# RWKV-7 attention and an exact-GELU MLP on one core: the first three chunks' a, v and r are turned on TensorE instead of VectorE, and the work ahead of the main loop is put in another order

## The chip, the cores and the metric

The kernel runs on one core of a Trainium2 chip. The time is device time in microseconds (us) of the whole launch; lower is better. Before the change it is 798.99 us, the median of 3 runs (798.1 to 800.18).

## The reference, cut to what matters

For each of 4 batches and 8 heads a 40 by 40 state is carried over 768 time steps; the result then goes through an MLP of width 2048.

```python
for t in range(S):                                   # S = 768, D = 40
    y[:, :, t] = einsum('bhd,bhde->bhe', rt, state)
    Sa = einsum('bhde,bhe->bhd', state, at)
    state = state * wt[:, :, None, :] - outer(Sa, bt) + outer(vt, kt)
x = y.transpose(0, 2, 1, 3).reshape(B * S, H * D)    # 3072 x 320
h = x @ w_in                                         # w_in 320 x 2048
out = gelu_exact(h) @ w_out                          # w_out 2048 x 320
```

## The kernel before, in words

Time is cut into 12 chunks of 64 steps (c = 0 to 11). In a chunk the recurrence is solved as matrix products over all 32 batch-heads: decays are accumulated (`sums`: cum, wT_ps), b and k are scaled by them (`scale_b` into nb, `scale_k` into ks), and then come the products of pairs of time steps: N from a and b, A from a and k, RV from r and v, M from r and the solved sa. Each is masked to its triangle by a VectorE multiplication out of PSUM (`masked`, L467). N needs an inverse of a triangular matrix. This is done in blocks of 32 (`start_inverse`): N is masked, written to DRAM by four DMAs (L504), read back in another layout by two (L547), inverted column by column by 62 small operations (L561, L562) on VectorE for chunk 0 and on GpSimd for the others, written to DRAM (`store_inverse`, L574) and read back (`fetch_inverse`, L584 and L588) into Tt and T2. Then `corner` (L, J) and `joined` (J2) complete the inverse; `make_X`, `make_sa`, `make_saT`, `make_M` and `make_QY` (QY) give the chunk's output and the next state, and `outputs` brings the output into the MLP's layout (xt) with eleven small DMAs.

The MLP of a chunk (`mlp`) is cut into eight pieces that `fill` puts between the steps of the next chunk's recurrence: four ph pieces (xt times w_in, L748, then GELU) and four po pieces (times w_out, L756).

Both weights come in 64-bit floats as pairs of 32-bit words, and are made into 32-bit floats on the chip (`to_float`, L263 to L282) piece by piece: five pieces for each half of w_in, sixteen for w_out. VectorE, ScalarE and GpSimd share a piece, or VectorE does most of it alone. `first_load` and `second_load` bring the words; `convert` and `seconds` put the pieces between other steps. The raw words lie in buffers that are needed later (w_out_sb, gt, spare_raw), so loads wait for conversions. The first two ph pieces need the first half of w_in, the next two the second half; the first po piece needs w_out's pieces 0 to 7.

All engines work their instructions in the order in which the program is written (`manual_schedule`); nothing reorders them. Chunks 0 to 2 are written out by hand ahead of the loop (L807 to L976), since they run beside the loading and the converting of the weights; chunks 2 to 11 then go through the loop of L978. DMAs are issued by the queue of SP or of ScalarE, also in program order: a DMA that waits holds back all that stands behind it on its queue.

The a, v and r of a chunk must be turned so that time runs along the free axis. Before, `fetch_pairs` (L146 to L162) loads them as pairs of steps in overlapping pieces of 72 and 48 elements, so that VectorE's 32 by 32 block transposes (`turn`, L164 to L167) give the turned form; that is four DMAs for a, eight for v and eight for r. v is loaded a second time as plain rows (`load_VR`, L181), for use as a right-hand side. b and k after scaling are turned on TensorE (`flip`, L387) and copied out of PSUM by ScalarE (L434, L446). The `warm` matmuls between steps (L801) compute nothing that is used.

Of the kernel before, what the change touches and what calls it, by code (L numbers as in the profile page):

```python
# [10 lines left out]
FP32 = mybir.dt.float32  # L11
UINT32 = mybir.dt.uint32
ALU = mybir.AluOpType
# [6 lines left out]
def kernel(  # L20
# [82 lines left out]
    def ring(name, n, shape, zero, eng):  # L103
        tiles = []
        for i in range(n):
            t = const.tile(shape, FP32, name=f"{name}{i}")
            if zero is not None:
                eng.memset(zero(t), 0.0)
            tiles.append(t)
        turn = [0]  # L110

        def take():
            turn[0] += 1
            return tiles[(turn[0] - 1) % n]
        return take
# [5 lines left out]
        return t  # L121


    def unused(t):
        for x in range(2):
            nc.gpsimd.memset(t[x * HP + BL:(x + 1) * HP, :, BW - BL:D + BL], 0.0)
# [3 lines left out]
    VR_ring = ring("VR", 2, [P, 2, G, NP, VC], None, None)  # L130


    raws = {}
# [30 lines left out]
    def turn(to, c, n):  # L164

        nc.vector.transpose(to.rearrange("p n (s y) -> p n y s", y=2),  # L166
                            raws.pop((c, n)).rearrange("p n (y d) -> p n y d", y=2)[:, :, :, :BL])  # L167

    def load_w(c, t=None, eng=nc.sync):
        t = w_tile if t is None else t  # L170
        fetch(c, "w", w, eng, t[:, :G * DM].rearrange("p (g h d) -> p g h d", g=G, h=H))
        raws[c, "w"] = t

    def load_a(c, t=None, eng=nc.sync):
        fetch_pairs(c, "a", a, eng, False, t)

    def load_kb(c):
        fetch(c, "b", b, nc.sync)
# [31 lines left out]
    load_w(1, early_w)  # L210
    fetch(1, "b", b, nc.sync, ahead["b"])
    load_a(1, early_a)
    for t in (*paired.values(), early_a):
        unused(t)

    one = const.tile([P, 1], FP32, name="one")
    nc.vector.memset(one, 1.0)
# [18 lines left out]
        nc.gpsimd.memset(wp_ring()[:, :, 0], 1.0)  # L236
    ks_ring, nb_ring = (ring(n, 2, [P, G, H, HP], pads, nc.gpsimd) for n in ("ks", "nb"))
    Tt_ring = ring("Tt", 1, [P, 2, G, NP, C], whole, nc.gpsimd)

    part_ring, avs_ring = (ring(n, 1, [P, 2, DM + REST], lambda t: t[:, :, DM:], nc.gpsimd) for n in ("part", "avs"))  # L240

    def flat(t):
        return t.rearrange("p j g n t -> p (j g n) t")
# [158 lines left out]
        return t.rearrange("p g n (e t) -> p g n e t", e=2)  # L402

    def turn_a(c):
        aT = turned_in.setdefault(c, {})["aT"] = work.tile([P, 2, G, NP, C], FP32, tag="aT", name="aT", bufs=2)
        turn(aT.rearrange("p e g i t -> p (e g i) t"), c, "a")

# [14 lines left out]

    def scale_a(c):
        t = turned_in[c]
        aT = t["aT"]
        wp = t["wp"].rearrange("p (n e) t -> p e n t", e=2)[:, :, :, :C]
        flat_a = aT.rearrange("p e g i t -> p e (g i) t")
        nc.vector.tensor_tensor(flat_a, flat_a, wp, ALU.mult)
        t["aT"] = aT.rearrange("p e g i t -> p g i e t")

    def turn_b(c):
# [17 lines left out]
    def turn_v(c):  # L449
        t = turned_in[c]  # L450
        vT = side("vT", "late", 1)
        turn(vT.rearrange("p q m (e t) -> p (q m e) t", e=2), c, "v")
        t["vT"] = parts(vT)

    def turn_r(c):
        rT = side("rT", "rT", 2)
        turn(rT.rearrange("p q m (e t) -> p (q m e) t", e=2), c, "r")
        turned_in[c]["rT"] = parts(rT)

    def turns_b(c):  # L460
# [5 lines left out]
    def masked(to, pt):  # L466
        nc.vector.tensor_tensor(to, pt, upper.unsqueeze(1).to_broadcast([P, 2 * G * NP, C]), ALU.mult)  # L467
# [37 lines left out]
                                  in_=flat(N)[at:at + BL, :, z * BL:(z + 1) * BL])  # L505
        blocks[c] = blk

    def make_RV(c):
        t = turned_in[c]
        masked(flat(t["VR"])[:, :, D:], products("RV_ps", t["vT"], t["rT"], False))  # L510

    def make_A(c, mask=True):
        t = turned_in[c]
# [299 lines left out]
    make_N(0)  # L813
    logs(1)
    sums(1)
    warm(3, 3)
    scale_b(1)
    turn_a(1)
    scale_a(1)
    inverse = start_inverse(0, nc.vector)  # L820
    turn_b(1)
    fetch(0, "k", k, nc.sync)
    for _ in range(5):
        next(inverse)
    make_N(1)
    scale_k(0)

    spare_x = work.tile([P, NK, TB], FP32, tag="xt", name="spare_x").rearrange("p k t -> p (k t)")
    st_ring()
# [1 line left out]
    spare_w = spare_st.rearrange("p e i g d -> p (e i g d)")  # L831
    nw = BL // 2 * BL
    run(start_inverse(1, nc.gpsimd, (spare_x[:, :BL * BL], spare_w[:, :nw], spare_w[:, nw:])))
    turn_k(0)
    make_A(0, False)
    fetch(1, "k", k, nc.sync, ahead["k"])
    load_w(2, None, nc.scalar)
    first_load(False, 0, early(0, 4))
    load_a(2, None, nc.scalar)
    fetch(2, "b", b, nc.scalar)  # L840
    load_v(0)
    load_r(0, nc.scalar)
    load_VR(0)
# [10 lines left out]
    turn_k(1)  # L854
    turn_r(0)
    make_RV(0)
    make_A(1, False)
    warm(4, 4, 4, 4)
    load_VR(1)
    first_load(True, 0, early(4))  # L860
    corner(0)
    warm(2)
    joined(0)
    warm(2)
    make_X(0)
    make_sa(0)
    mask_A(1)
    make_saT(0)
    warm(2)
    first_pieces((0, 1, 2), 0, nc.gpsimd)  # L870
    convert(1)
    make_y2(0)
    make_M(0)
    first_load(False, 2, early(5, 4))
    store_inverse(1)
    fetch_inverse(1)
    nc.gpsimd.memset(spare_st.rearrange("p e i g d -> p (e i g) d")[:, :, D:], 0.0)
    convert(1, True)
    warm(2)
    make_QY(0)  # L880
    outputs(0)
    pieces.append(mlp(0))
    make_av(1)
    convert(1)
    first_pieces((3,), 0, nc.vector)
    first_pieces((4,), 0, nc.gpsimd)
    corner(1)
    turn_state()
    convert(1)
    joined(1)  # L890
    convert(1, True)
    make_X(1)
    sums(2)

    first_load(False, 3)
    for f in range(4):
        second_load(f, 2 * f)
    first_load(True, 1, spare_raw[:, :LW])
    make_sa(1)
    make_saT(1)  # L900
    scale_b(2)
    turn_a(2)
    scale_a(2)
    first_pieces(range(NK), 1, nc.gpsimd)
    convert(1)
    fill()
    turn_b(2)
    convert(1)
    load_r(1)
    load_v(1)  # L910
    fetch(2, "k", k, nc.sync)
    convert(1)
    fill()
    make_N(2)
    convert(1)
    turn_r(1)
    make_y2(1)
    make_M(1)
    convert(1, True)
    turn_v(1)  # L920
    make_RV(1)
    for f in range(4, 8):
        second_load(f, 2 * f)
    scale_k(2)
    run(start_inverse(2, nc.gpsimd))
    second_load(8, 0, spare_raw)
    second_load(9, 2, spare_raw)

# [6 lines left out]
    make_QY(1)  # L935
    outputs(1)
    pieces.append(mlp(1))
    load_VR(2)
    load_v(2)
    load_r(2)  # L940
    load_w(3)
    seconds(6)
    turn_v(2)
    turn_r(2)
    make_RV(2)
    make_A(2)
    fill()
    load_a(3)
    load_kb(3)
    seconds(0, (10, 12))  # L950
    make_av(2)
    logs(3)
# [2 lines left out]
    turn_a(3)  # L955
    scale_a(3)
    turn_state()
    load_VR(3)
    load_v(3)
    load_r(3)  # L960
    seconds(1, (11, 14))
    fill()
    seconds(1, (12, 0, spare_raw), (13, 2, spare_raw))
# [2 lines left out]
    fetch_inverse(2)  # L966
    seconds(2, (14, 14))
    seconds(1, (15, 0, spare_raw))
    seconds(2, last=True)
    fill()  # L970
    make_N(3)
# [92 lines left out]
```

## Time and profile before

| | us |
|---|---|
| median of 3 runs | 798.99 |
| the profiled execution, whole | 802.02 |
| its span (first to last instruction) | 800.3 |
| TensorE busy in the span | 697.4 |
| VectorE, ScalarE, GpSimd busy | 280.3, 214.5, 312.0 |

The profiled execution lies 3.0 us above the median; 1.7 us of it lie outside the span. In the profile PE is TensorE's matmuls, PEld its weight loads, DVE VectorE, ACT ScalarE, POOL GpSimd; SPq and ACTq are the queues of SP and ScalarE that issue DMAs. A line such as L467 is a line of the kernel. A timeline row gives start, duration, engine, line, operation, the tile written and the tile read, with the number of instructions merged into it; in square brackets is the idle time ahead of it and what ended that. The granted TensorE clock is a share of full speed.

### The profile page before, as it was taken

What the parts mean: (1) busy time and instruction counts of PE and PEld (TensorE: products, weight loads), DVE (VectorE), ACT (ScalarE), POOL (GpSimd) and SP (SyncE); (2) the same over time, 40 slices, a digit from 0 to 9 for tenths busy, and PEclk for the clock granted to TensorE, in tenths of its full rate; (3) what the DMA queues carried; (4) which work ended last, traced back from release to release, by engine and by line L of the source; (5) the groups of instructions that cost most, each with busy time, mean ns of one, the idle gap of its engine ahead of it and who ended that gap; (6) DMA issues with size and microseconds to landing.
All of it is one profiled execution on the core that took longest, in us unless ns stands there. A gap on an engine that the chain in (4) does not pass through costs nothing.

```text
span 800.3 us, 30351 instructions
## 1 busy us (share of the span) xinstructions
PE 697.4 (87%) x13666; PEld 557.9 (70%) x13666; DVE 280.3 (35%) x425; ACT 214.5 (27%) x258; POOL 312.0 (39%) x778
## 2 busy tenths in 40 slices
PE   7207774628599999999999999999999999999997
PEld 4205664525388788787887887877878878878684
DVE  3742646584612414314234124143142341311000
ACT  5112453214123233134232332331332322102020
POOL 4183326841056066074281470650742824700000
PEclk9659786958699999999999999999999999999999
DMA  8798375086372472553643724724635432020100
GB/s 129 131 159 168 70 180 145 19 135 132 83 136 50 73 137 55 106 99 67 120 79 66 142 52 72 138 57 93 111 69 115 82 68 51 17 51 2 26 9 17
DMA packets 275178, 70.28 MB, mean 88 GB/s; under 512 B 263432, under 2 KB 268328, under 8 KB 275048
## 3 DMA queue, kind: packets, MB, share of 16 engines
q1 hardware_dynamic: 264032, 66.24, 43.4%
q10 hardware_dynamic: 11016, 2.10, 1.7%
q8 instruction: 107, 1.75, 0.9%
q14 instruction: 23, 0.19, 0.1%
HBM read 54.13 MB, written 10.22 MB: 80 GB/s over the span
## 4 chain that ended last, share of the span: by engine, by line
PE 80%; DMA 6%; DVE 4%; SPq 4%; issue 2%; ACT 2%; DVEq 0%; ACTq 0%
PE ph L748 27%; PE po L756 26%; PE QY L100 6%; PE J L100 2%; PE sap L100 2%; PE RV_ps L100 2%; PE M_ps L100 2%; PE saT_ps L100 2%; PE av L100 2%; PE N_ps L100 1%; PE kT_ps L392 1%; PE A_ps L100 1%; PE cum L100 1%; PE X L100 1%; DMA b_raw<-in_b_dram 1%
## 5 line engine op out<-in xcount | busy, mean ns | idle before, releaser
L756 PE MATMUL po<-w_out_sb,gt 128*128 128x320 f32 x768 | 223.2, 444 | 11.2 <-DVE w_out_sb L276 9.4
L748 PE MATMUL ph<-xt,w_in_sb 64*128 64x256 f32 x1920 | 223.2, 384 | 2.6 <-issue 2.5
L748 PEld LDWEIGHTS ph<-xt,w_in_sb 64*128 64x128 f32 x1920 | 185.2, 189 | 25.8 <-issue 4.1
L756 PEld LDWEIGHTS po<-w_out_sb,gt 128*128 128x128 f32 x768 | 144.5, 194 | 73.2 <-DVE w_out_sb L276 13.2
L561 POOL TENSOR_TENSOR tmp<-W,Nb 128x126 f32<-128x126 f32 (+22 forms) x310 | 112.2, 362 | 171.9 <-DMA Nb<-N 148.3
L562 POOL TENSOR_TENSOR W<-W,tmp 128x126 f32<-128x126 f32 (+22 forms) x310 | 117.0, 377 | 24.3
L750 ACT ACTIVATE gt<-ph 128x1024 f32<-128x1024 f32 x48 | 49.1, 1024 | 166.7 <-PE ph L748 166.6
L760 DVE COPY os<-po 128x320 f32<-128x320 f32 x24 | 11.8, 492 | 109.5 <-PE po L756 109.5
L467 DVE TENSOR_TENSOR SM<-M_ps,upper 128x1024 f32<-128x1024 f32 x12 | 14.7, 1225 | 74.3 <-PE M_ps L100 74.3
L100 PE MATMUL RV_ps<-rT,vT 40*64 40x64 f32 x768 | 15.6, 236 | 25.9 <-DVE rT L166 21.5
L705 DVE TENSOR_TENSOR xt<-QY,wpT 128x512 f32<-128x512 f32 x24 | 15.5, 686 | 61.5 <-PE QY L100 61.5
L100 PE MATMUL av<-VR,A 64*64 64x40 f32 x768 | 14.4, 234 | 24.9 <-DVE A L467 24.9
L417 POOL TENSOR_TENSOR ks<-k_raw,part 128x640 f32<-128x640 f32 x10 | 16.2, 1624 | 50.7 <-DMA r_pairs<-in_r_dram 20.4
L545 POOL MEMSET W<- 128x512 f32 x10 | 5.3, 530 | 74.9 <-DMA inv<-W 74.9
L100 PEld LDWEIGHTS av<-VR,A 64*64 64x64 f32 x768 | 13.1, 142 | 29.5 <-DVE A L467 25.1
L100 PEld LDWEIGHTS RV_ps<-rT,vT 40*64 40x64 f32 x768 | 13.9, 149 | 27.8 <-issue 26.4
L627 DVE COPY Tt<-J 32x512 f32<-32x512 f32 x12 | 8.3, 689 | 71.3 <-ACT Tt L627 71.3
L446 ACT COPY kT<-kT_ps 128x1024 f32<-128x1024 f32 x12 | 12.1, 1012 | 71.3 <-PE kT_ps L392 71.3
L467 DVE TENSOR_TENSOR VR<-RV_ps,upper 128x1024 f32<-128x1024 f32 x12 | 14.7, 1224 | 46.9 <-PE RV_ps L100 46.9
L268 ACT ACTIVATE power<-power,rebias 128x320 uint32<-128x320 uint32 (+1 forms) x26 | 16.2, 624 | 49.2 <-DVE power L267 49.2
L467 DVE TENSOR_TENSOR A<-A_ps,upper 128x1024 f32<-128x1024 f32 x12 | 14.7, 1223 | 39.9 <-PE A_ps L100 39.9
L529 ACT COPY avs<-av 128x640 f32<-128x640 f32 x12 | 8.3, 694 | 64.7 <-PE av L100 58.3
(136 smaller groups left out, 881.1 us busy)
## 6 DMA issues: line engine op xcount, KB each, us to landing
Nb<-N SPq DMA_DIRECT2D x22, 256.0 KB
VR<-in_v_dram SPq DMA_DIRECT2D x24, 160.0 KB
out_dram<-os SPq DMA_DIRECT2D x48, 80.0 KB
k_raw<-in_k_dram SPq DMA_DIRECT2D x22, 160.0 KB
w_out_sb<-in_moe_w_out_dram SPq DMA_DIRECT2D x11, 320.0 KB
v_pairs<-in_v_dram SPq DMA_DIRECT2D x48, 72.0 KB
w_tile<-in_w_dram SPq DMA_DIRECT2D x20, 160.0 KB
b_raw<-in_b_dram SPq DMA_DIRECT2D x20, 160.0 KB
```

Of the source, the lines that this page charges most:

```text
L100: nc.tensor.matmul(o, lhsT, rhs, start=first, stop=True, skip_group_check=True)
L268: nc.scalar.activation(power, power, ACT.Relu, bias=rebias, scale=8.0)
L417: eng.tensor_tensor(ks[:, :, :, :D], raws.pop((c, "k")), rwv, ALU.mult)
L446: nc.scalar.copy(kT, flip(by_pair(t["ks"]), "kT_ps"))
L467: nc.vector.tensor_tensor(to, pt, upper.unsqueeze(1).to_broadcast([P, 2 * G * NP, C]), ALU.mult)
L561: eng.tensor_tensor(t, views[0], views[1], ALU.mult)
L562: eng.tensor_tensor(views[2], views[2], t, ALU.add)
L705: nc.vector.tensor_tensor(xt[:, :NP, g * P:(g + 1) * P].rearrange("p i (e t) -> p i e t", e=2), Y, wp[:, g, :, :, :C], ALU.mult)
L748: nc.tensor.matmul(ph[:, x, s], w_in_sb[half(x), kt, p * P:(p + 1) * P], xt[half(x), kt], start=kt == 0, stop=kt == NK - 1)
L750: nc.scalar.activation(gt[:, 4 * q:4 * q + 4].rearrange("p (x s) t -> p x s t", x=2), ph, ACT.Gelu)
L756: nc.tensor.matmul(po[:, g], gt[:, f, g * P:(g + 1) * P], w_out_sb[:, f], start=f == 0, stop=f == NF - 1)
L760: nc.vector.tensor_copy(os, po[:, g])
```

## The change

For chunks 0 to 2 (`NT = 3`) a and r are loaded as plain rows, padded to 64 columns a head, and turned by `flip` on TensorE; v is not loaded a second time, but turned on TensorE from the rows that `load_VR` brings (16 matmuls with the identity). a's scaling by the decay reads PSUM directly; v and r are copied out of PSUM by ScalarE. r of chunk 1 goes into v's buffer. The zeroing of columns that this needs is done on GpSimd at the start, and the old buffers' unused parts are zeroed later (`unused`: four memsets on GpSimd, two on VectorE).

The steps ahead of the loop are put in another order: k of chunks 0 and 1 is loaded with w, b and a at the start; chunk 1's N is masked before the first inverse's columns rather than after five of them; r, v rows and w of the next chunks go to SP's queue instead of ScalarE's; A and RV of chunk 0 are multiplied before the first inverse ends, and masked after it; the loads of w_in, the conversions, and chunk 1's and 2's v and r stand at other places. Of the ten `warm` matmuls one stays, of 384 columns.

```diff
+    NT = 3
     def load_a(c, t=None, eng=nc.sync):
-        fetch_pairs(c, "a", a, eng, False, t)
+        if c < NT:
+            fetch(c, "a", a, eng, by_64(paired["a"] if t is None else t).rearrange("p (g h) d -> p g h d", g=G))
+        else:
+            fetch_pairs(c, "a", a, eng, False, t)
...
     def load_v(c):
-        fetch_pairs(c, "v", v, nc.sync, True)
+        if c >= NT:
+            fetch_pairs(c, "v", v, nc.sync, True)
 
     def load_r(c, eng=nc.sync):
-        fetch_pairs(c, "r", r, eng, True)
+        if c >= NT:
+            fetch_pairs(c, "r", r, eng, True)
+            return
+        t = by_64(paired["v" if c == 1 else "r"]).rearrange("p (h g) d -> p h g d", g=G)
+        for e in range(2):
+            for g in range(G):
+                eng.dma_start(out=t[half(e), :, g, :D],
+                              in_=r[G * e + g, :, c * C:(c + 1) * C].rearrange("h t d -> t h d"))
+        raws[c, "r"] = t
...
     load_a(1, early_a)
+    fetch(0, "k", k, nc.sync)
+    fetch(1, "k", k, nc.sync, ahead["k"])
...
     def turn_v(c):
+        if c < NT:
+            pt = duo("vT_ps").rearrange("p q (m t) -> p q m t", m=NP)
+            for q in range(2):
+                for m in range(NP):
+                    for g in range(G):
+                        mm(pt[half(g), q, m], t["VR"][:, g, q, m, :HP], ident)
+            nc.scalar.copy(vT, pt)
...
     def turn_r(c):
+        if c < NT:
+            raw = raws.pop((c, "r"))
+            nc.scalar.copy(rT, flip(lambda q, m: raw[:, NP * q + m].rearrange("p g d -> p (g d)"), "rT_ps"))
...
     run(inverse)
     queues = nc.sync, nc.scalar
     store_inverse(0, queues)
+    load_VR(1)
+    first_pieces((0,), 0, nc.vector)
+    convert(1)
     fetch_inverse(0, queues)
-    first_load(False, 1)
-    turn_v(0)
-    scale_k(1, nc.vector)
     mask_A(0)
+    mask_RV(0)
     make_av(0)
...
+    load_w(3)
+    load_kb(3)
+    load_VR(3)
+    unused(paired["r"], nc.vector)
+    load_a(3)
+    seconds(6)
     fill()
```

Three places where the order of instructions moves. First SP's queue, from behind chunk 1's second transfer of N (spare_x) to the first inverse's write (inv). This is how it stands before; w_out_sb is here the raw buffer of w_in's words, and SP has only one of the two inv transfers, ScalarE's queue has the other:

```order
L143 DMA early_k<-in_k_dram 64x16x40 x2
L330 DMA w_out_sb<-in_moe_w_in_dram 64x4x512
L330 DMA w_out_sb<-in_moe_w_in_dram 64x3x512
L332 DMA w_out_sb<-in_moe_w_in_dram 40x512
L333 DMA w_out_sb<-in_moe_w_in_dram 24x512
L158 DMA v_pairs<-in_v_dram 32x8x72 x2
L158 DMA v_pairs<-in_v_dram 32x8x48 x2
L158 DMA v_pairs<-in_v_dram 32x8x72 x2
L158 DMA v_pairs<-in_v_dram 32x8x48 x2
L184 DMA VR_70<-in_v_dram 64x16x40 x2
L574 DMA inv<-W 1024x1x32
```

The same queue in the changed kernel, between the same two transfers:

```order
L191 DMA VR_131<-in_v_dram 64x16x40 x2
L204 DMA r_pairs<-in_r_dram 64x8x40 x4
L144 DMA w_tile<-in_w_dram 64x16x40 x2
L353 DMA w_out_sb<-in_moe_w_in_dram 64x4x512
L353 DMA w_out_sb<-in_moe_w_in_dram 64x3x512
L355 DMA w_out_sb<-in_moe_w_in_dram 40x512
L356 DMA w_out_sb<-in_moe_w_in_dram 24x512
L353 DMA w_out_sb<-in_moe_w_in_dram 64x4x512
L353 DMA w_out_sb<-in_moe_w_in_dram 64x3x512
L355 DMA w_out_sb<-in_moe_w_in_dram 40x512
L356 DMA w_out_sb<-in_moe_w_in_dram 24x512
L622 DMA inv<-W 1024x1x32
```

The eight small loads of v pairs are gone, r and w have come over from ScalarE's queue, and a second group of w_in's words stands in front of the inverse's write; before, that group stood behind its read.

Second, VectorE behind the first inverse's last column (W). Before:

```order
L562 TENSOR_TENSOR W<-W,tmp 128x16
L166 STREAM_TRANSPOSE vT<-v_pairs 128x16x2x32
L417 TENSOR_TENSOR ks_130<-early_k,avs_140 128x16x40
L467 TENSOR_TENSOR A<-A_ps,upper 128x1024
L166 STREAM_TRANSPOSE rT<-r_pairs 128x16x2x32
L467 TENSOR_TENSOR VR_70<-RV_ps,upper 128x16x64
L597 STREAM_TRANSPOSE L<-Tt_136 128x512
```

In the changed kernel:

```order
L610 TENSOR_TENSOR W<-W,tmp 128x16
L290 TENSOR_SCALAR power<-w_out_sb 128x512
L292 TENSOR_SCALAR mant<-w_out_sb 128x512
L509 TENSOR_TENSOR A<-A_ps,upper 128x1024
L509 TENSOR_TENSOR VR_131<-RV_ps,upper 128x16x64
L295 SCALAR_TENSOR_TENSOR power<-w_out_sb,power 128x512
L298 SCALAR_TENSOR_TENSOR mant<-w_out_sb,mant 128x512
L299 SCALAR_TENSOR_TENSOR w_in_sb<-mant,power 128x512
L509 TENSOR_TENSOR A<-A_ps,upper 128x1024
L645 STREAM_TRANSPOSE L<-Tt_129 128x512
```

The transposes and chunk 1's scaling of k are gone from here, and a conversion of w_in stands in two parts around chunk 0's masks; it reads the words of both groups of loads above.

Third, VectorE from chunk 1's output (xt, st) to chunk 2's masks (VR, A), where w_out's pieces (power, mant) stand. The seven rows below are the changed kernel's; before, six pieces and the two transposes of v and r stood between the last st row and the VR row:

```order
L753 TENSOR_TENSOR xt<-QY,wpT_118 128x4x128 x2
L775 TENSOR_TENSOR st_74<-QY,st_72 128x8x40
L776 TENSOR_TENSOR st_74<-st_74,wpT_118 128x8x40
L775 TENSOR_TENSOR st_74<-QY,st_72 128x8x40
L776 TENSOR_TENSOR st_74<-st_74,wpT_118 128x8x40
L509 TENSOR_TENSOR VR_131<-RV_ps,upper 128x16x64
L509 TENSOR_TENSOR A<-A_ps,upper 128x1024
```

The masks come first now, and the six pieces behind them; on TensorE the first po piece of chunk 0 still stands directly behind chunk 2's A.

More of the change, by code (lines that the diff above doesn't have):

```diff
@@ L404, in turn_a @@
     def turn_a(c):
+        if c < NT:
+            turned_in.setdefault(c, {})["a_ps"] = flip(by_pair(raws.pop((c, "a"))), "aT_ps")
+            return
         aT = turned_in.setdefault(c, {})["aT"] = work.tile([P, 2, G, NP, C], FP32, tag="aT", name="aT", bufs=2)
@@ L815 @@
     sums(1)
-    warm(3, 3)
+    scale_k(0)
+    inverse = start_inverse(0, nc.vector)
     scale_b(1)
@@ L819 @@
     scale_a(1)
-    inverse = start_inverse(0, nc.vector)
+    warm(3)
     turn_b(1)
-    fetch(0, "k", k, nc.sync)
-    for _ in range(5):
-        next(inverse)
+    scale_k(1)
     make_N(1)
-    scale_k(0)
     spare_x = work.tile([P, NK, TB], FP32, tag="xt", name="spare_x").rearrange("p k t -> p (k t)")
@@ L833 @@
     run(start_inverse(1, nc.gpsimd, (spare_x[:, :BL * BL], spare_w[:, :nw], spare_w[:, nw:])))
+    load_VR(0)
+    load_r(0)
+    load_w(2)
+    first_load(False, 0, early(0, 4))
+    first_load(False, 1)
     turn_k(0)
     make_A(0, False)
[L836 to L843, printed above, removed]
+    turn_v(0)
+    turn_r(0)
+    make_RV(0, False)
+    turn_k(1)
     logs(2)
@@ L903 @@
     scale_a(2)
-    first_pieces(range(NK), 1, nc.gpsimd)
     convert(1)
@@ L919 @@
     convert(1, True)
[L920 to L924, printed above, removed]
+    for n in "av":
+        unused(paired[n], nc.gpsimd)
     run(start_inverse(2, nc.gpsimd))
+    load_VR(2)
+    load_r(2)
     second_load(8, 0, spare_raw)
```

106 lines of the change are left out of this document (56 added, 50 removed).

## The prediction

> **What bounds the kernel now.** I first read the page, to see where TensorE is not busy.
>
> ```profile
> span 800.3 us, 30351 instructions
> PEclk9659786958699999999999999999999999999999
> PE 80%; DMA 6%; DVE 4%; SPq 4%; issue 2%; ACT 2%; DVEq 0%; ACTq 0%
> ```
>
> Four fifths of the chain that ended last are TensorE, and its granted clock is full in all slices but the first eleven. Next I cut the span into stages (us from the start; busy us and instructions of PE, PEld, DVE, ACT, POOL; granted clock; DMA share; GB/s). The cuts are where TensorE begins chunk 0's av (58.8), ends chunk 0's QY (87.5), begins chunk 1's sap (103.2), begins the third ph piece (138.4), ends chunk 1's QY (152.9), begins chunk 2's av (184.3) and ends chunk 3's turning of k (219.5).
>
> ```profile
> 25.00:58.80 33.80, 3.99 (x76) 3.40 (x76) 21.96 (x67) 3.03 (x3) 18.36 (x45) 0.50 0.88 148
> 58.80:87.50 28.70, 23.63 (x684) 18.24 (x684) 9.88 (x14) 7.32 (x12) 12.26 (x27) 0.82 0.73 138
> 87.50:103.20 15.70, 8.42 (x332) 7.01 (x325) 12.61 (x18) 6.83 (x12) 6.09 (x5) 0.89 0.44 95
> 103.20:138.40 35.20, 22.32 (x472) 20.23 (x472) 18.14 (x23) 17.11 (x24) 13.51 (x12) 0.74 0.62 151
> 138.40:152.90 14.50, 14.32 (x221) 12.05 (x216) 6.44 (x14) 4.50 (x6) 12.29 (x31) 0.92 0.12 44
> 152.90:184.30 31.40, 9.88 (x146) 7.54 (x146) 23.21 (x40) 3.37 (x6) 15.62 (x36) 0.62 0.69 120
> 184.30:219.50 35.20, 22.86 (x254) 15.16 (x254) 19.73 (x44) 11.52 (x15) 2.98 (x4) 0.75 0.45 98
> 219.50:794.40 574.90, 572.82 (x11221) 462.61 (x11220) 158.77 (x196) 148.51 (x168) 222.13 (x590) 1.00 0.40 75
> ```
>
> From 219.5 us on TensorE is busy for 572.8 of 574.9 us. The change edits nothing behind that point, so what counts is how much earlier chunk 3's turning of k ends. Ahead of it TensorE waits (waits of TensorE up to 220 us: total, times, longest):
>
> ```profile
> PE av L100 <- DVE A L467: 24.9, 1, 24.9
> PE RV_ps L100 <- DVE rT L166: 21.5, 1, 21.5
> PE po L756 <- DVE w_out_sb L276: 9.4, 5, 5.7
> PE QY L100 <- DVE rT L166: 6.4, 1, 6.4
> PE RV_ps L100 <- DVE vT L166: 4.4, 1, 4.4
> ```
>
> Four of the five name VectorE's work on chunks 0 to 2, and the change touches these four.
>
> **Step 1, to the first J.** The timeline around the first inverse:
>
> ```profile
> 21.91 1.16 PE L100 MATMUL N_ps<-aT,nT 40*64 40x64 f32 x64 [1.16 <-DVE W L548]
> 24.89 0.19 DVE L561 TENSOR_TENSOR tmp<-W,Nb 128x31 f32<-128x31 f32 x1 [3.02 <-DMA Nb<-N]
> 27.24 1.22 DVE L467 TENSOR_TENSOR N<-N_ps,upper 128x1024 f32<-128x1024 f32 x1
> 31.94 1.29 SPq L547 DMA_DIRECT2D spare_x<-N  x2
> 42.45 10.14 SPq L158 DMA_DIRECT2D v_pairs<-in_v_dram  x8
> 45.50 0.19 DVE L562 TENSOR_TENSOR W<-W,tmp 128x16 f32<-128x16 f32 x1
> 54.29 0.56 ACTq L574 DMA_DIRECT2D inv<-W  x1
> 55.47 1.25 DVE L166 STREAM_TRANSPOSE vT<-v_pairs 128x1024 f32<-128x1024 f32 x1 [9.78 <-DMA v_pairs<-in_v_dram]
> 58.85 0.85 SPq L584 DMA_DIRECT2D Tt<-inv  x2
> 64.74 0.70 DVE L597 STREAM_TRANSPOSE L<-Tt 128x512 f32<-128x512 f32 x1
> 64.69 3.70 PE L100 MATMUL warm<-cum_m,ident 128*128 128x512 f32 x8
> 68.32 0.45 PE L100 MATMUL J<-L,N 32*32 32x32 f32 x31
> ```
>
> W is ready at 45.7, but SP issues v pairs until 52.6, and the write goes out at 54.3: 8.6 us lost. Then come 4.6 us to the read, 5.9 to L, 0.7 for L and 2.9 behind warm matmuls: 22.6 us from W to J.
>
> In the changed kernel the inverse starts about as early. The two k's are 640 KB ahead of N; two a's shrink by 160 KB each, so 320 KB more are ahead, 1.6 us at 207 GB/s (below) if DMA ends last there, nothing if it doesn't; I take 0.5. The 62 operations took 20.8 us with a mask of 1.2 in between; that mask now comes first, leaving 19.6. GpSimd now runs its own inverse beside most of it, not only the last 6 us. The w_out pieces further down show such company making VectorE dearer. I add 0 to 4 and take 2: W at 47.
>
> But the order puts two groups of w_in's words in front of the write, and VectorE, behind W, reads both before it masks A. What SP then has behind chunk 1's N: spare_x 512 KB, v, r and w 320 each, twice 1024 of words: 3520 KB, or 3.6 MB. N's product is done at 23.1, so its mask now ends at 24.3 rather than 28.5, and spare_x is read at about 27.9 rather than 31.9. For the rate one stretch serves, and as the slow end the 148 GB/s of the stage from 25 to 58.8:
>
> ```profile
> 35.00:40.00 5.00, 0.00 (x0) 0.00 (x0) 4.49 (x16) 0.00 (x0) 0.30 (x2) 0.50 1.28 207
> ```
>
> At 207 GB/s the words are there 17.4 us after about 28.9, at 46.3; at 148, at 53. Of the two I take 180, between them since these are rows of 160 bytes and of 2 KB in turn: 49. So the new wait costs 2 us behind W, with nothing queued that TensorE could use earlier. Then on one side two conversion operations, the masks of A and RV, av, chunk 1's A and its mask; on the other the inverse's write and read, 4.6 and at most 5.9 (VectorE was busy when that read landed). Both sides end near 57.5; L, and J at about 58.5. **Ten us earlier** (5 to 13).
>
> At this place the Trainium skill bears on the loads. Its page "DMA: Bandwidth & Descriptors" (section "Specifications") says that transfers below 512 bytes a piece are slow. The stretch at 207 GB/s mixes pieces of 160 to 2048 bytes and no row separates them, so by that page the sum would lean to the 148 end, a loss of 4 us.
>
> **Step 2, J to chunk 0's QY.** 68.3 to 87.5 is 19.2 us before, the same steps after. Conversions stand between them now as then; six warm matmuls are gone. I give 2 us: QY ends 12 earlier. If the lower clock costs more, nothing.
>
> **Step 3, chunk 1 to sap.**
>
> ```profile
> 39.62 0.25 POOL L561 TENSOR_TENSOR st<-st,spare_x 128x31 f32<-128x31 f32 x1 [10.09 <-DMA spare_x<-N]
> 67.13 0.23 POOL L562 TENSOR_TENSOR st<-st 128x16 f32<-128x16 f32 x1
> 76.06 1.27 SPq L574 DMA_DIRECT2D inv<-st  x2
> 83.09 1.93 SPq L584 DMA_DIRECT2D Tt<-inv  x4
> 10.18 1.06 PE L392 MATMUL nT_ps<-ident,nb 128*128 128x128 f32 x8 [0.65 <-POOL rebias L258]
> 11.29 1.01 ACT L434 COPY nT<-nT_ps 128x1024 f32<-128x1024 f32 x1 [0.66 <-PE nT_ps L392]
> ```
>
> GpSimd's inverse takes 27.7 us and is done at 67.4, yet SP issues its write only at 76.1, behind weights; the read comes 7.0 later. Now it starts at 33 to 36 and ends near 62, but its write still stands behind weight loads and r: I put it at 66.5, the read at 73.5, 9.5 earlier. Behind L TensorE now does v and r before J2. A flip of eight costs 1.06 and its copy 1.01. For v's sixteen full matmuls of 128 columns no row exists: the warm row gives 0.23 for 128 columns, so 3.7 if they go one by one; the flip is the low end; I take 1.9, since the two halves of the array can take one each as in the small products. Nothing hides these 3 us, and the copies another 1. But from reading Tt to sap were 20.1 us before, of which a conversion on VectorE took part; it goes behind. **sap 9 us earlier** (5 to 12).
>
> **Step 4, sap to the third ph piece**, 35.2 us before.
>
> ```profile
> 138.44 5.65 PE L748 MATMUL ph<-xt,w_in_sb 64*128 64x256 f32 x40
> 184.29 1.14 PE L100 MATMUL av<-VR,A 64*64 64x40 f32 x64
> 217.56 1.97 PE L392 MATMUL kT_ps<-ident,ks 128*128 128x128 f32 x8
> 156.12 0.55 DVE L267 TENSOR_SCALAR power<-w_out_sb 128x320 uint32<-128x320 uint32 x1
> 171.22 0.49 DVE L276 SCALAR_TENSOR_TENSOR w_out_sb<-mant,power 128x320 f32<-128x320 f32 x1
> ```
>
> The waits for rT and vT (6.4 and 4.4) go, since both are turned before. RV itself, 2 us, goes ahead of sap. 35.2 less 12.8 is 22.4. What ends last then is w_in's second half, five pieces through three engines; I give it 2.6 more: 25. **The third ph piece comes at 119, 19.4 earlier.** From there to the end of QY nothing is saved: TensorE is busy for 14.3 of 14.5 us.
>
> **Step 5, chunk 1's QY to chunk 2's av**, 31.4 before: xt and st, six pieces (156.1 to 171.7, 15.6 us, 2.6 each), two transposes, RV, A, po. Of the wait of 21.5 us the pieces are the larger part; it is no loading time. Now the flips and copies of v and r run beside xt and st: 4.2 us; RV 1.2 (as N's product), its mask 1.2, A's mask 1.2, two small memsets for which I put 0.9, slack 0.3: 9. Then the six pieces, which the first po piece needs: 15.6, or 3 less if GpSimd's inverse ends meanwhile; then 0.5 for the last po matmuls. That is 25: **6.4 saved**, TensorE's wait moving from RV to po.
>
> **Step 6, av to k of chunk 3**: the same steps, the same waits for w_out's last pieces; r and v of chunk 3 go to the end of SP's queue there, 16 issues, each 1.3 us at worst by the row of the eight v pairs, ahead of chunk 3's N. TensorE has po pieces to do meanwhile, so I take nothing; with that cover gone it would be 5.
>
> **Sum**: 19.4 and 6.4 are 25.8, call it 26. 802.0 for the profiled execution becomes 776; the median of the runs shown is 3.0 below that, so I forecast **773.0**.
>
> **The rivals.**
> *Weights bind.* In stage 4 the conversions kept their own pace (17 to 18 us of VectorE and ScalarE, 13.5 of GpSimd in 35.2) and the five pieces need all of it. Then stage 4 yields nothing and the third ph piece is only 9 earlier; with step 5's 6.4 about 15: 784. For it: the three engines wait on each other's parts. Against: none is busy for more than about half. Chance 0.22.
> *All goes well.* Words at 207 GB/s (3 more), stage 4 at its floor (2.6), step 5 without GpSimd's company (3): 35 saved, 764. Chance 0.11.
> *The change doesn't do what it says.* The inverse's transfers are said to be in front of the weights; the order shows a group more in front of the write. If words come at 148 GB/s, J gains 5 and the whole 21: 778, inside my range, counted with the forecast.
> *Slower: TensorE stays cold.* Nine warm matmuls go. In the stage from 25 to 58.8, with 4.0 of 33.8 us busy, the clock was 0.50; with warm matmuls, 0.82. If it stayed 0.50 up to chunk 3, busy time would grow by (clock/0.5 - 1) in each stage: 15 + 7 + 11 + 12 + 2 + 11 = 58 us. From 26 of these on the path the gain is gone; with 36, 809. Against it: from 138.4 to 152.9 the clock is 0.92 with no warm matmul, only ph's own. The Trainium skill states the rule ("TensorE: Matmul & The Clock Gate", Part 1): half rate after an idle window of about 3.4 us, full after a busy one of about 3.4. By it ph pieces of 4 to 6 us still warm the array, as that stage shows. Chance 0.06.
> *No difference*, gains lost to several waits: 0.03. The forecast itself 0.58.
>
> **How the numbers follow.** The likeliest case is 773.0, from 766 to 781 by its own bounds. Down to 761 lies the case where all goes well, up to 788 most of weights bind; outside are slower, no change and tails, under 0.2. Faster 0.91, within 0.3% (2.4 us, about what a measurement here can tell) 0.03, slower 0.06.
>
> **What would show it.** Right: the inverse's write near 47 to 49 and J before 61; sap near 94; the third ph near 119; TensorE waiting for po and not for RV; a dense TensorE from about 193. Wrong: VectorE idle before A's mask until 55 or later; the third ph later than 129; the granted clock below 0.6 from 95 to 125; or idle TensorE behind chunk 3's k, so that the gain isn't carried to the end.

## The result, and the profile after

The changed kernel takes 780.25 us, the median of 4 runs (778.21 to 783.0); the kernel before, run beside it, 799.59 (798.1 to 800.72, 4 runs). The ratio is 0.9761, with a 95% interval from 0.9726 to 0.9797: 19.3 us faster. Its profiled execution, 778.21 us, is the fastest of the four, and that of before, 802.0, lies above its median; so the two traces differ by 24 us where the medians differ by 19.3.

The page of the changed kernel:

```profile
span 776.1 us, 30554 instructions
PEclk9666897867999999999999999999999999999999
PE 81%; DVE 4%; DMA 4%; issue 4%; SPq 3%; POOL 2%; ACT 1%; POOLq 0%; DVEq 0%; ACTq 0%
```

The clock is 0.9 or more from the eleventh slice on; the slices before it are the part the change edits. The same stages as in the table of before, cut at the same events (us from the start; busy us and instructions of PE, PEld, DVE, ACT, POOL; granted clock; DMA share; GB/s):

```profile
25.00:54.00 29.00, 8.19 (x173) 7.24 (x167) 22.89 (x66) 5.79 (x6) 16.81 (x44) 0.65 0.88 144
54.00:78.50 24.50, 16.98 (x640) 15.53 (x636) 18.43 (x23) 9.48 (x16) 14.42 (x26) 0.65 0.77 140
78.50:95.40 16.90, 12.93 (x372) 11.21 (x374) 6.22 (x11) 4.89 (x6) 1.24 (x1) 0.80 0.56 118
95.40:123.40 28.00, 19.61 (x441) 16.19 (x436) 15.38 (x20) 16.73 (x25) 14.90 (x11) 0.92 0.62 161
123.40:137.80 14.40, 14.01 (x200) 11.42 (x200) 4.35 (x11) 4.01 (x5) 12.05 (x33) 0.81 0.37 73
137.80:161.50 23.70, 14.67 (x191) 8.03 (x184) 19.75 (x40) 5.41 (x8) 15.70 (x37) 0.75 0.69 117
161.50:197.40 35.90, 23.77 (x254) 16.01 (x254) 19.71 (x44) 11.54 (x15) 2.98 (x4) 0.69 0.39 88
197.40:770.00 572.60, 570.85 (x11219) 461.99 (x11218) 158.74 (x196) 148.77 (x168) 223.58 (x590) 1.00 0.40 75
```

The gain sits ahead of 197.4 us, where TensorE now becomes dense (219.5 before). Two rows matter below: from 78.5 to 95.4 VectorE, ScalarE and GpSimd are mostly idle, and from 95.4 to 123.4 TensorE is busy for 19.6 of 28.0. The waits of TensorE up to 215 us (total, times, longest):

```profile
PE po L804 <- DVE w_out_sb L299: 17.2, 11, 5.6
PE vT_ps L100 <- DMA VR<-in_v_dram: 10.2, 1, 10.2
PE av L100 <- DVE A L509: 9.5, 1, 9.5
PE ph L796 <- POOL w_in_sb L304: 6.1, 2, 3.5
PE J L100 <- DVE L L645: 5.9, 2, 4.0
```

The 24.9 us in front of av are 9.5, and the waits for VectorE's rT and vT are gone. At the top stand po's wait for w_out, as forecast, and a load of chunk 0's v. That load costs nothing here: behind the work that it holds up TensorE waits 9.5 us more, for A's mask. By events (us):

| event | before | forecast | after |
|---|---|---|---|
| write of the first inverse | 54.3 | 47 to 49 | 48.9 |
| first J | 68.3 | 58.5 | 60.3 |
| end of chunk 0's QY | 87.5 | 75.5 | 76.0 |
| chunk 1's sap | 103.2 | 94 | 95.4 |
| end of the third ph piece | 144.1 | 124.7 | 129.1 |
| chunk 2's av | 184.3 | 158.5 | 161.5 |
| end of chunk 3's turning of k | 219.5 | 193.5 | 197.4 |

The timeline around the first inverse:

```profile
17.23 2.40 SPq L546 DMA_DIRECT2D N<-N  x4
26.39 0.19 DVE L609 TENSOR_TENSOR tmp<-W,Nb 128x31 f32<-128x31 f32 x1 [2.64 <-DMA Nb<-N]
48.65 0.19 DVE L610 TENSOR_TENSOR W<-W,tmp 128x16 f32<-128x16 f32 x1
48.86 0.56 SPq L622 DMA_DIRECT2D inv<-W  x1
51.46 0.46 DVE L290 TENSOR_SCALAR power<-w_out_sb 128x512 uint32<-128x512 uint32 x1 [2.62 <-DMA w_out_sb<-in_moe_w_in_dram]
59.54 0.70 DVE L645 STREAM_TRANSPOSE L<-Tt 128x512 f32<-128x512 f32 x1
60.29 1.08 PE L100 MATMUL J<-L,N 32*32 32x32 f32 x64 [1.97 <-DVE L L645]
```

The write leaves as W is done, and the new wait of 2.6 us for words stands behind W. Then, in the same view, the parts that fell short: the turnings of v and r in chunks 0 to 2 (chunk 0's r is left out), the third ph piece with GpSimd's first and last step of w_in's second half, and VectorE's idle time before chunk 1's xt.

```profile
35.90 3.68 PE L100 MATMUL vT_ps<-ident,VR 128*64 128x128 f32 x32 [10.16 <-DMA VR<-in_v_dram]
82.67 3.68 PE L100 MATMUL vT_ps<-ident,VR 128*64 128x128 f32 x32
86.28 1.93 PE L415 MATMUL rT_ps<-ident,v_pairs 128*128 128x128 f32 x8
99.08 1.29 POOL L303 TENSOR_TENSOR mant<-mant,gt 128x512 f32<-128x512 f32 x1 [19.34 <-ACT mant L302]
114.71 1.57 PE L796 MATMUL ph<-xt,w_in_sb 64*128 64x256 f32 x12
119.80 1.23 PE L796 MATMUL ph<-xt,w_in_sb 64*128 64x256 f32 x4 [3.52 <-POOL w_in_sb L304]
122.32 1.26 POOL L304 TENSOR_TENSOR w_in_sb<-mant,power 128x512 f32<-128x512 f32 x1
123.63 5.49 PE L796 MATMUL ph<-xt,w_in_sb 64*128 64x256 f32 x24 [2.61 <-POOL w_in_sb L304]
137.80 1.29 DVE L753 TENSOR_TENSOR xt<-QY,wpT 128x512 f32<-128x512 f32 x2 [9.73 <-PE QY L100]
137.84 1.97 PE L100 MATMUL vT_ps<-ident,VR 128*64 128x128 f32 x32
139.74 1.09 PE L415 MATMUL rT_ps<-ident,r_pairs 128*128 128x128 f32 x8
```

The same turnings took 3.68 and 1.93 us in chunk 1 and 1.97 and 1.09 in chunk 2. The granted clock was 0.50 and 0.54 in chunk 1's two (82.7 to 86.3 and 86.3 to 88.2), and 1.00 from 137.8 to 139.7.

GpSimd had been idle for 19.3 us when it began these five pieces at 99.1, and it ends the last at 123.6, where the ph piece goes on.

### The profile page after: what moved, and what is told of

It reads as the page before. It is cut to its first block, busy times and chain, and to the rows that moved or that the text cites. A ratio compares the mean times of both kernels' runs of the same rounds, so it can differ in the third digit from the quotient of the medians.

```text
span 776.1 us, 30554 instructions
## 1 busy us (share of the span) xinstructions
PE 701.0 (90%) x13792; PEld 561.1 (72%) x13792; DVE 273.7 (35%) x419; ACT 220.0 (28%) x262; POOL 313.0 (40%) x779
## 4 chain that ended last, share of the span: by engine, by line
PE 81%; DVE 4%; DMA 4%; issue 4%; SPq 3%; POOL 2%; ACT 1%; POOLq 0%; DVEq 0%; ACTq 0%
PE ph L796 27%; PE po L804 26%; PE QY L100 6%; PE J L100 2%; PE av L100 2%; PE sap L100 2%; PE cum L100 2%; PE saT_ps L100 2%; PE N_ps L100 2%; DMA w_out_sb<-in_moe_w_in_dram 1%; PE RV_ps L100 1%; PE X L100 1%; PE A_ps L100 1%; PE kT_ps L415 1%; PE nT_ps L415 1%
## 5 line engine op out<-in xcount | busy, mean ns | idle before, releaser
L804 PE MATMUL po<-w_out_sb,gt 128*128 128x320 f32 x768 | 225.0, 445 | 18.9 <-DVE w_out_sb L299 17.2
L593 POOL MEMSET W<- 128x512 f32 x10 | 5.3, 531 | 73.5 <-DMA inv<-W 73.4
L100 PEld LDWEIGHTS QY<-SM,nb 64*64 64x64 f32 x768 | 18.7, 140 | 5.1 <-issue 3.6
L100 PE MATMUL QY<-SM,nb 64*64 64x104 f32 x768 | 21.2, 262 | 1.3 <-DVE SM L509 1.3
```

The costliest lines, as they stand in the source:

```text
L100: nc.tensor.matmul(o, lhsT, rhs, start=first, stop=True, skip_group_check=True)
L804: nc.tensor.matmul(po[:, g], gt[:, f, g * P:(g + 1) * P], w_out_sb[:, f], start=f == 0, stop=f == NF - 1)
```

## The experiments

My theory: the gain is that of the forecast's steps, and what is missing went to w_in's second half (step 4), to the dearer turning of v (step 3) and to the words in front of the masks (step 1). The rivals: the turning alone or the order alone makes the gain; the colder array takes it; chunk 1's inverse, not the conversions, sets step 4. Edits are against the changed kernel unless said; ratios are to the kernel before.

**The two halves of the change.** First the new order with VectorE turning:

```diff
-    NT = 3
+    NT = 0
     load_VR(0)
+    load_v(0)
     load_r(0)
-    turn_v(0)
-    turn_r(0)
-    make_RV(0, False)
...
     store_inverse(0, queues)
+    turn_v(0)
+    turn_r(0)
+    make_RV(0, False)
```

with `load_v(1)` and `load_v(2)` beside `load_r`, and the memsets of before.

> The new order of loads and work, but a, v and r of chunks 0 to 2 turned by VectorE from paired rows as before (v and r of chunk 0 are turned behind the inverse's write, or the inverse would wait for them). Theory 1, the gain is mostly the turning (v and r no longer stand on VectorE and their eight small issues of 1.3 us no longer stand on SP): SP issues v's and r's pairs ahead of the weights, 20 us more, so the inverse's write goes out near 60 instead of 48.9 and the waits for rT and vT behind chunk 1's and 2's work come back; 800 us or more, ratio 1.00 or above. Theory 2, the gain is mostly the order: J stays before 63 and the time is near 785, ratio 0.982.

Then the old order with TensorE turning: the program of before from `logs(0)` on, with the changed helpers and memsets and `NT = 3`.

> The old order with TensorE turning a, v and r of chunks 0 to 2 (rows loaded as in the changed kernel; k, weights, warm matmuls and the inverse's transfers where they were). Theory 1, mostly the turning: SP has no 10.1 us of v pairs in front of the inverse's write, VectorE doesn't wait 9.8 us for them, and the waits of TensorE for rT and vT (21.5, 6.4 and 4.4 us) shrink; 787 us, ratio 0.985, two thirds of the gain of 19.3. Theory 2, mostly the order: chunk 1's mask of N stands in the inverse and the inverse of chunk 1 is written late as before, so no more than 6 us come, 794, ratio 0.993.

Measured: the order alone 793.41 us, 0.9906 (0.9885 to 0.9927); the turning alone 796.13 us, 0.9942 (0.9920 to 0.9964). TensorE's waits in chunks 0 and 2, in front of RV with the order alone, and then in front of v's turning with the turning alone:

```profile
52.31 1.99 PE L100 MATMUL RV_ps<-rT,vT 40*64 40x64 f32 x64 [24.93 <-DVE rT L167]
156.20 1.99 PE L100 MATMUL RV_ps<-rT,vT 40*64 40x64 f32 x64 [5.80 <-DVE rT L167]
```

```profile
54.10 3.60 PE L100 MATMUL vT_ps<-ident,VR 128*64 128x128 f32 x32 [20.74 <-DMA VR<-in_v_dram]
166.88 3.53 PE L100 MATMUL vT_ps<-ident,VR 128*64 128x128 f32 x32 [13.25 <-DMA VR<-in_v_dram]
```

Neither half carries the change: 0.94% and 0.58% make 1.5%, together they are 2.4%. The first row of each pair is chunk 0, where TensorE waited 24.9 us for A's mask before: with the order alone it waits as long for VectorE's rT, with the turning alone 20.7 us for the load of v. So the wait ahead of the first J only changes its name, and J is at 65.3 and 72.3 us (68.3 before, 60.3 with both). The second rows are chunk 2, where the wait for rT was 21.5: the order alone cuts it to 5.8. From chunk 1's QY to chunk 2's av the order alone takes 24.7 us and the turning alone 29.4; before it was 31.4, and it is 23.6 with both. So step 5 is nearly all the order's, and the steps up to the first J need both. For the order, both theories missed the time (1.00 and 0.982), though the inverse's write left at 57.6, near the 60 of the first; for the turning the second's time held.

**The first inverse and the words in front of it.** Can J's step be had earlier by putting the inverse before the words, or the masks before the conversion?

```diff
     first_load(False, 0, early(0, 4))
-    first_load(False, 1)
...
-    first_pieces((0,), 0, nc.vector)
-    convert(1)
     fetch_inverse(0, queues)
+    first_load(False, 1)
...
     joined(0)
+    first_pieces((0,), 0, nc.vector)
+    convert(1, True)
```

> The changed kernel with the second group of w_in's words issued behind the first inverse's write and read, and the first conversion behind chunk 0's joined inverse, so VectorE goes from the inverse straight to the masks. Theory 1, the wait for words is on the path: the masks end 5 us earlier, J comes at 56 to 57 instead of 60.3, and 3 us of it reach the end: 777 us, ratio 0.972. Theory 2, the conversions bind later: J comes earlier by as much but the third ph piece stands still at 123.6 for its last 28 matmuls, and the time is 780, ratio 0.976, or above since the words come later.

Measured: 786.58 us, 0.9824 (0.9803 to 0.9845), slower than the change. J came at 59.6 only, so the run tests neither theory. Moving the conversion changed another wait: in the trace's records the turning of chunk 1's k now waits for a semaphore of VectorE too, where it waited for one of GpSimd alone, and ScalarE's half of the write, at 52.9 instead of 48.9, stood behind the copy of that k. The timeline:

```profile
50.68 1.94 PE L415 MATMUL kT_ps<-ident,ks 128*128 128x128 f32 x8 [7.14 <-POOL st L609]
```

The releaser named is not the one: A's mask on VectorE ended at 50.5, and k's turning starts 0.1 later. That its accumulator is now one that this mask frees is likely, but no record names it. So for the next runs chunk 1's k is turned right behind chunk 0's A. The first of them moves only the conversion:

```diff
     make_A(0, False)
+    turn_k(1)
...
-    turn_k(1)
...
-    first_pieces((0,), 0, nc.vector)
-    convert(1)
     fetch_inverse(0, queues)
     mask_A(0)
     mask_RV(0)
+    first_pieces((0,), 0, nc.vector)
+    convert(1)
```

> The changed kernel with VectorE's first conversion behind chunk 0's two masks instead of in front of them, and chunk 1's k turned right behind chunk 0's A, so that it needs no accumulator that A's mask frees (the wait that spoiled the run before). Words and transfers stand where they are. Theory 1, the wait for words in front of the masks is a cost on the path: the masks end 3.5 us earlier, L is then set by the inverse's read, J comes at 58 instead of 60.3 and 2 us reach the end: ratio 0.974. Theory 2, L needs the read anyway: J within 1 us of 60.3, ratio 0.976.

Measured: 782.84 us, 0.9770 (0.9739 to 0.9801). J came late, at 64.4. The inverse had begun 1.5 us later than in the changed kernel's trace, and there is a new wait: the conversion's step on ScalarE is queued behind ScalarE's read of the inverse, and VectorE, which has L behind that conversion, waits for it. SP's half of the write is late too, at 53.4 where ScalarE's leaves at 50.6; the next run shows why. ScalarE's timeline:

```profile
57.95 0.96 ACTq L632 DMA_DIRECT2D Tt<-inv  x2
59.55 0.72 ACT L291 ACTIVATE power<-power,rebias 128x512 uint32<-128x512 uint32 x1 [14.79 <-POOL st L609]
```

The same with `fetch_inverse(0, queues)` behind `convert(1)`:

> As the run with the masks first, but with the first conversion between the masks and the inverse's read in program order, so that its step on ScalarE is not queued behind ScalarE's read of the inverse (that cost 6.5 us of VectorE there). Theory 1, the wait for words in front of the masks costs what it says: VectorE saves 2.6 us there and J comes 1 to 2 us before 60.3, ratio 0.974. Theory 2, L is set by the inverse's read, which itself waits on SP for words to land: J stays within 1 us of 60.3 and the ratio is 0.976.

Measured: 779.92 us, 0.9744 (0.9719 to 0.9768), as the change. The masks did end 3.2 us earlier (51.6, not 54.8), but J came at 59.8. The timeline from the write to L, and SP's longest wait from 30 to 62 us:

```profile
49.37 0.63 ACTq L622 DMA_DIRECT2D inv<-W  x1
52.13 0.56 SPq L622 DMA_DIRECT2D inv<-W  x1
58.98 0.71 DVE L645 STREAM_TRANSPOSE L<-Tt 128x512 f32<-128x512 f32 x1 [2.77 <-DMA Tt<-inv]
```

```profile
SPq L622 <- DMA inv<-W: 8.8, 1, 8.8
```

SP held its half of the write until ScalarE's half had landed, since both now use one DMA semaphore (number 108 in the trace's records; in the changed kernel 108 and 109). So L got its read late. The second theory's time held, for another reason than it gave. And the words behind the read, as in the first of these runs, with chunk 1's k turned early and both masks in front:

> As the run with the masks first, and the second group of w_in's words is issued behind the first inverse's write and read; the first conversion goes behind chunk 0's second J. Theory 1, the words cost the inverse its transfers (the write landed 3.8 us after its issue with them in front): J at 56 instead of 60.3, but the words come about 9 us later, at 62 to 63, conversions of w_in start that much later, QY of chunk 0 still comes no sooner than now because its conversions stand on VectorE in front of the masks of M and the outputs: ratio 0.976 to 0.980, nothing won. Theory 2, the words have slack: the 4 us are kept to the end, ratio 0.971.

Measured: 783.49 us, 0.9787 (0.9761 to 0.9814). J and chunk 0's QY:

```profile
57.04 1.08 PE L100 MATMUL J<-L,N 32*32 32x32 f32 x64 [3.37 <-DVE L L645]
75.98 2.96 PE L100 MATMUL QY<-VR,ks 64*64 64x104 f32 x64
```

J is 3.3 us earlier and QY ends 2.9 later, at 78.9: theory 1. The words are needed by the conversions ahead of QY, so putting them behind the inverse gives its gain back. What an earlier J brings with the words unmoved stays open; each edit that tried it made another wait.

**The colder array.** The warm matmuls of before at their old places: `warm(4, 4, 4, 4)` behind chunk 1's A, `warm(2)` behind both J, behind saT and ahead of QY.

> The changed kernel with the warm matmuls of before at their old places from chunk 1's A to chunk 0's QY. Theory 1, the colder array costs nothing there that counts, since the stage waits for VectorE: the granted clock rises above 0.8 from 54 to 78, but J comes up to 3 us later behind the warm matmuls and the ratio is 0.976 to 0.981. Theory 2, the cold clock (0.65 in that stage) is what step 2 lost: QY of chunk 0 ends 3 to 5 us earlier and the ratio is 0.971.

Measured: 780.2 us, 0.9745 (0.9719 to 0.9771), no difference that can be told. The stage from 54.0 to 78.5:

```profile
54.00:78.50 24.50, 20.15 (x566) 13.83 (x562) 15.46 (x20) 8.87 (x15) 13.05 (x26) 0.85 0.82 144
```

The clock rose from 0.65 to 0.85, J came 2.2 us later, QY ended within a us of 76.0: theory 1, though two effects cancel here. QY's products started 1.6 us later and took 3.2 us instead of 4.4. So the run doesn't show that a low clock is free, only that these matmuls cost what they give. At the end of this stage VectorE decides: in the changed kernel chunk 0's xt starts at 78.5, behind a conversion and 2.5 us behind QY's end. Chunk 1's turning of v, behind this stage, took 3.68 us in this run too.

**w_in's second half.** Its five conversions begin at 81 us, with the transfers that this needs:

```diff
     load_r(1)
+    store_inverse(1)
...
-    store_inverse(1)
+    first_load(False, 3)
+    fetch_inverse(1)
     load_a(2)
     fetch(2, "b", b, nc.sync)
-    fetch_inverse(1)
-    first_load(False, 3)
...
     corner(1)
+    first_pieces(range(NK), 1, nc.gpsimd)
+    convert(2)
     turn_v(1)
     turn_r(1)
     joined(1)
+    convert(1)
...
-    first_pieces(range(NK), 1, nc.gpsimd)
-    convert(1)
```

Two of the five stand behind `corner(1)` now, one behind `joined(1)`, and the last two behind `scale_a(2)` and `turn_b(2)`.

> The changed kernel with the five pieces of w_in's second half begun from 81 us on, where VectorE, ScalarE and GpSimd are mostly idle (6.2, 4.9 and 1.2 us busy of 16.9), instead of from 94 us on; for that the last words are issued ahead of chunk 1's inverse read, chunk 1's inverse is written behind r, and a and b of chunk 2 go behind its read. Theory 1, these pieces are what step 4 lost: TensorE's wait for GpSimd before the third ph piece (6.1 us) goes, the third ph piece's last matmuls start near 116 instead of 123.6, ratio 0.968. Theory 2, the stage is then bound by chunk 2's N and M, or the pieces delay chunk 1's own copies, so that the third ph piece gains 2 us or none: ratio 0.974 to 0.977.

And the first half of that diff alone, the transfers:

> Of the run with w_in's second half early only the transfers: the last words ahead of chunk 1's inverse read, chunk 1's inverse written behind r, a and b of chunk 2 behind its read; the five conversions stay where they are in the changed kernel. Theory 1, the gain there came from the conversions' earlier start: chunk 1's sap comes at most 2 us before 95.4, the third ph piece's last matmuls keep waiting for GpSimd near 122 to 124, ratio 0.974 to 0.976. Theory 2, it came from chunk 1's inverse and the words: ratio 0.968 or below.

Measured: 771.47 us, 0.9631 (0.9604 to 0.9658), with the conversions; 780.55 us, 0.9754 (0.9727 to 0.9782), with the transfers alone. GpSimd's first and last step and the third ph piece, with the conversions early, and then the piece with the transfers alone:

```profile
84.39 1.40 POOL L303 TENSOR_TENSOR mant<-mant,gt 128x512 f32<-128x512 f32 x1 [5.17 <-ACT mant L302]
108.35 1.28 POOL L304 TENSOR_TENSOR w_in_sb<-mant,power 128x512 f32<-128x512 f32 x1
112.64 4.59 PE L796 MATMUL ph<-xt,w_in_sb 64*128 64x256 f32 x40
```

```profile
118.46 1.22 PE L796 MATMUL ph<-xt,w_in_sb 64*128 64x256 f32 x4 [3.79 <-POOL w_in_sb L304]
122.29 4.32 PE L796 MATMUL ph<-xt,w_in_sb 64*128 64x256 f32 x24 [2.61 <-POOL w_in_sb L304]
```

With the conversions early the piece runs through and ends at 117.2 instead of 129.1; chunk 3's k ends 10 us earlier, at 187.4. With the transfers alone the piece still waits for GpSimd and ends at 126.6. So step 4 was bound by the start of the five conversions: theory 1 in both runs.

**w_out's pieces.** Three of six go into VectorE's 9.7 idle us:

```diff
-    seconds(1)
+    seconds(4)
     fill()
     make_QY(1)
...
-    seconds(6)
+    seconds(3)
```

> The changed kernel with three of the six w_out pieces in front of chunk 1's xt instead of behind chunk 2's masks: VectorE is idle there for 9.7 us. Theory 1, the pieces are the wait of step 5: TensorE's wait for po falls by three pieces of 2.3 us, chunk 2's av begins 6 to 7 us earlier, 774 us, ratio 0.968. Theory 2, beside GpSimd's inverse of chunk 2 the pieces grow past the hole and delay xt, or the scalar engine's part of them waits behind its own work: no gain, 780 or above, ratio 0.976 or above.

Measured: 776.34 us, 0.9695 (0.9670 to 0.9720): theory 1. From the end of chunk 1's QY (141.1) to chunk 2's av:

```profile
139.48 1.61 PE L100 MATMUL QY<-VR,ks 64*64 64x104 f32 x64
141.97 1.27 DVE L753 TENSOR_TENSOR xt<-QY,wpT 128x512 f32<-128x512 f32 x2
159.08 1.95 PE L100 MATMUL av<-VR,A 64*64 64x40 f32 x64
```

That is 18.0 us where the change has 23.6; xt waits 1 us for the pieces. av itself comes only 2.4 us before that of the change's trace, since this execution was already 3.5 us behind at chunk 1's sap, where the edit changes nothing; the gain of 0.7% rests on the medians. Both early parts together, and these with the masks first:

> The run with w_in's second half early and, as in the run with w_out early, three of the six w_out pieces in front of chunk 1's xt. Theory 1, the two waits lie behind each other and add up: from chunk 1's QY to chunk 2's av falls from 25.6 to about 19, the ratio is 0.956 to 0.957 (0.963 less the 0.0066 that the w_out pieces gave alone). Theory 2, with the third ph piece earlier the six pieces' words or GpSimd's inverse are in the way: 0.960 or above.

> The three edits together: w_in's second half early, three w_out pieces early, masks first. Theory 1, the masks' gain comes on top: 0.954 to 0.955. Theory 2, the masks' edit is worth nothing: the same as without it, 0.956 to 0.957.

Measured: 765.13 us, 0.9559 (0.9535 to 0.9583), and 766.16 us, 0.9567 (0.9541 to 0.9593). Over the change the two early parts give 1.3% and 0.7% alone and 2.1% together: they add up, as forecast. The masks' edit adds nothing, but it had the same hindrance: SP's half of the write left 4.1 us behind ScalarE's, again on one semaphore. The first of the two has the lowest time of all, 36 us below the kernel before, though the two can't be told apart.

## Why the prediction was right, and where it was off

The sign and the mechanism were right: the inverse's write left as W was done, TensorE's waits for VectorE's rT and vT went, and the gain was carried to the dense part. The time, 780.25, lies in the range, but 7.25 above the forecast: the medians gained 19.3 us of the 26 that the sum gave. Of this 2.2 is the sum: 776 was forecast for the profiled execution and it took 778.2. The other 5 is the step from that execution to the median: I took 3.0 off, as for before, and here the median is 2.0 above.

*Step 1, 10 forecast, 8.0 measured.* Words were put at 49 and came at 51.5:

```profile
28.80:51.50 22.70, 7.23 (x112) 6.39 (x112) 18.29 (x54) 5.07 (x5) 14.70 (x39) 0.65 1.00 167
```

The last column is 167 GB/s where I took 180. Of this 149 is the rate up to 36.6, where SP issued spare_x and the rows of 160 bytes, and 176 the rate behind it, where it issued the words. The Trainium skill's page "DMA: Bandwidth & Descriptors" (section "Specifications") says that pieces below 512 bytes do not reach the full rate; the trace agrees by direction, though the whole stretch doesn't come down to the 148 end. GpSimd's company made the columns take 22.4 us instead of 19.6 (2 was allowed). The inverse began 1.0 later than I said, since N's write stood behind both k's on SP until 17.2. So W was done at 48.8, where I said 47. L followed chunk 1's mask of A without a wait, so the masks' side ended last, but only just: by the trace's semaphore records the last part of the read that L needs landed at 58.9, 0.7 before L began. The two sides ended nearly together, as I had it, and both were late, one by the words and one by W; without the words' wait alone J would have come 0.7 earlier at most.

*Step 2, 12 forecast, 11.5 measured*: right as a number, by luck. J to the end of QY took 15.8 us, 3.4 less than before where I gave 2, and that made good most of what step 1 lost. Why it was shorter than that, I leave open. The lower clock that I feared made QY's products 1.2 us longer than in the run with the warm matmuls, but nothing waited for them: chunk 0's xt began only 2.5 us after QY's end.

*Step 3, 9 forecast, 7.8 measured.* The mis-sized term is the turning: 1.9 for v and 1.06 for r became 3.68 and 1.93, 2.65 more between J and sap. The sizes were right for a full clock, as chunk 2's 1.97 and 1.09 show; what I left out is that chunk 1's turning would run at half of it, behind the 4.0 us in which TensorE waited for L. How much of this reaches the end no run separates: VectorE's first conversion of step 4, at 94.3, stands behind the mask of chunk 1's RV, which needs that turning, so by these rows I estimate up to 2.65 us. The read of chunk 1's inverse was also later than I put it (77.5, not 73.5), behind the issues of a and b of chunk 2.

*Step 4, 10.2 of its own forecast, 7.2 measured*: the step that failed. I saw that the five w_in pieces end last but gave them 2.6 us over the floor. They ended at 123.6, 28.2 behind sap, against the 25 I gave the stage, and they hold the piece in its middle. The rival *weights bind* had named this and gave it the whole 10 us. The run with the conversions early shows its cause: they were started late, with three engines mostly idle before.

*Step 5, 6.4 forecast, 7.8 measured*, with the wait for po as forecast; the run with the w_out pieces confirms that these pieces are the term, and the run with the order alone that the new order makes the gain. *Step 6*: 0.7 lost, nothing forecast.

The steps make 22.1 us; the spans differ by 24.2. The 2.1 that come behind 197.4 have no step, and I leave them open: one pair of executions, within what runs of one kernel differ by (778.2 to 783.0 for the change). The same goes for the single steps, each read off one trace; what steps 4 and 5 wait for was tested by medians too.

*Slower: TensorE stays cold* didn't come as a whole: the stages from 54 on have a clock of 0.65 to 0.92, and raising it from 54 to 78.5 by warm matmuls left the time the same. In one place it did: chunk 1's turning at 0.50.

## What to carry to other kernels

When a stage ends on a chain of conversions through three engines, look at when the chain starts, not at how busy the engines are: moved into an idle stretch 15 us earlier, the same work gave 10 us. Two edits that remove the same wait from two sides are worth little alone, since the other side keeps it; measure them together. And an edit that moves one instruction can also move an accumulator or a DMA semaphore: read the waits at the new place before the time is taken as the price of the move.

## What the runs showed of the hardware

Beside GpSimd's two-input operations VectorE's simple ones get longer. Two steps of the same form, and GpSimd beside the second:

```profile
64.68 0.42 DVE L292 TENSOR_SCALAR mant<-w_out_sb 128x512 uint32<-128x512 uint32 x1
68.04 1.33 POOL L304 TENSOR_TENSOR w_in_sb<-mant,power 128x512 f32<-128x512 f32 x1
68.17 1.49 DVE L292 TENSOR_SCALAR mant<-w_out_sb 128x512 uint32<-128x512 uint32 x1
```

0.42 us became 1.49, and both end within 0.3 us. The Trainium skill, "GPSIMD Engine Reference" (section "1. Specifications"), says that GpSimd's way into SBUF is shared with VectorE; the trace agrees.

Sixteen matmuls of 128 columns into one half of the output partitions each (v's turning) took 1.97 us at a granted clock of 1.00. The warm row of before, four matmuls of 512 columns into all of the partitions, is as many columns and took 3.70 us, also at 1.00 (the rows count each of these matmuls twice, x32 and x8). So the two halves of the array ran side by side. At 0.50 the sixteen took 3.68 us: taken for a time at full clock, that looks like one by one. So the granted clock of that very stretch has to be read beside such a row.
